# Two layers of linear attention and two of gated units on one core: a third quarter of outputs by seven products, the last z in the gated units, z reciprocals for two tiles

## The chip, the cores and the metric

The kernel runs on one core of a Trainium2 chip. The metric is the device time of one execution in microseconds, as a median of runs. TensorE (PE in the profile) multiplies matrices into PSUM banks, VectorE (DVE), ScalarE (ACT) and GpSimd (POOL) work element by element, and SyncE (SP) issues most transfers.

## What is computed

The input x is 2048 rows of 1024 numbers. Two kinds of layer follow each other, twice: attention, gated units, attention, gated units, here layers 0, 1, 2 and 3. Layers 0 and 2 share their weights, so do 1 and 3.

```
def _A_ref(x, wqkv, wo):                     # 32 heads of 32
    qkv = (x @ wqkv) ...
    phi = lambda t: where(t > 0, t + 1, exp(t)) + 1e-6
    pq, pk = phi(q), phi(k)
    kv = einsum("bhsd,bhse->bhde", pk, v)
    z = einsum("bhsd->bhd", pk)
    o = (pq @ kv) / (pq . z + 1e-6)
    return o @ wo
def _B_ref(x, W_gate, W_up, W_down):
    return (relu(x @ W_gate) * (x @ W_up)) @ W_down
x = x + A(layernorm(x)); x = x + B(layernorm(x)); and both once more
```

## The kernel before

The 2048 rows are 16 tiles of 128, in four quarters of four tiles (QT is 4). Everything stays in SBUF where it can: a pool "big" of 16 slots holds weights, transposed activations and sums, "ep" has 7 temporaries, and PSUM's eight banks are "ps" (4, tag a), "ps3" (2, tag b) and "kvp" (kv0, kv1).

**Seven products.** Most matrix products are cut into two by two blocks and made from seven block products instead of eight (1: a11 b11, 5: s1 with a difference of b, 2, 6, 7, 3, 4). The sums s and the differences are made by VectorE in f16; a product is accumulated in PSUM on top of an earlier one, after VectorE or ScalarE has read that (L1154 for the gated units: v, x, y, z banks; L677 for q and k in layer 2; L843 for outputs).

**Attention.** After q, k and their phi (L435 relu, L436 exp on ScalarE, L439 the join on VectorE) comes the product of keys and inputs (m_products, L575), z_row, and kv folded with wo into T (fold_wo, L759). An output unit (out_unit, L776) is one tile by 512 columns: eight matmuls of 512 columns into a ps bank, which VectorE adds to x (add_up, L768). The quarters 0, 1 and 2 are made in 24 such units, `out0` and the loop over sc. The fourth quarter (sc 3) is made by out_pairs, seven products for two pairs of tiles, behind the third unit (u = 2) of the next layer. Each product there has two halves of four matmuls, one for each tile of a pair: after product 1 ScalarE copies X to Y (L847), after the others VectorE adds the bank to x (onto, L836, or add_up).

**z.** For each tile GpSimd multiplies pq with zrow (z_mult, L723), VectorE sums over heads, adds and inverts (z_sum, L728 to L730, 32 numbers a row), GpSimd scales pq in place (z_scale, L735), and SP transposes it by DMA into pqT (q_turn, L744). z_mult writes ksum, one buffer. Tiles 0 to 10 run as a chain, 11 to 15 at fixed ticks.

**Layer norms.** In layers 1 and 3, ln_norm_sums takes the mean from add_up's accumulators (L222, VectorE), then ScalarE does Square, Ln and Exp (L225 to L227), a shift and the scaling (L230, L231); the result is transposed by DMA (L410), and sums_x (L1127 to L1130, VectorE) makes four sums a tile, which product 5, 6, 3 and 7 of the first gated unit read. In layer 2, ln_root is Ln and Exp (L173, L174) and ln_scale is on VectorE (L180).

**Gated units.** glu makes one of 14 units of a chunk (two quarters) from fourteen block products (7 for gate, 7 for up), 56 matmuls. six adds z = y + m5 (L1190), then V (L1203), put (L1165) multiplies relu(gate) by up, and GpSimd makes one of the four blocks (L1207). In layer 1's first chunk make_gu makes the weights' differences on VectorE (L1064, L1066, L1067) and stores them from ScalarE's queue.

**What sets the order.** Work beside the matmuls is put in by a clock of its own: `later.at(n, f)` runs f after n more `later.tick()`, and there is a tick after each unit or product. The compiler's scheduler then orders each engine by the written order as priority, by when it thinks that inputs are ready; `issue_after` and `behind(it, ...)` put an instruction behind another of its engine. In the second half of an attention layer `manual_schedule` fixes VectorE's and GpSimd's order as written. The weight ring loads ahead through SP: load_to(index + 5) at each unit's start.

Of the kernel before, what the change touches and what calls it, by code (L numbers as in the profile page):

```python
# [8 lines left out]
ALU = mybir.AluOpType  # L9
# [83 lines left out]
class _Net:  # L93
    def __init__(self, tc, ctx, x_d, wqkv_d, wo_d, wg_d, wu_d, wd_d, out_d):
# [23 lines left out]
        self.small = pool("small", 4)  # L118
        self.ps = pool("ps", 4, space=PSUM)
# [64 lines left out]
    def ln_norm(self, layer, t):  # L184
# [14 lines left out]
        def scale(rstd=None if layer == 2 else rstd):  # L199
            if rstd is None:  # L200
                rstd = self.ln_root(mv)
                return lambda: scale(rstd)
# [12 lines left out]
    def ln_norm_sums(self, layer, t):  # L215
# [13 lines left out]
        def scale():  # L229
            nc.scalar.activation(out=shift, in_=mean, func=ACT.Identity, scale=rstd[:, 0:1])  # L230
# [181 lines left out]
    def ln_at(self, delay, layer, t, lag, after=None):  # L412
        def stat():
            with self.tc.issue_after(after) if after else nullcontext():
                scale = self.ln_norm(layer, t)
            self.later.at(1, lambda: norm(scale))
# [14 lines left out]
    def phi(self, ps, out):  # L431
# [4 lines left out]
        nc.scalar.activation(out=e, in_=e, func=ACT.Exp, scale=-1.0, bias=self.eps6[:, 0:1])  # L436
# [30 lines left out]
    def layer_A(self, l, last_ln):  # L467
# [248 lines left out]
        def z_chain(i):  # L716
            z_mult(*divmod(i, QT))
            if i < 10:
                later.at(2 + i % 2, lambda: z_chain(i + 1))

        def z_mult(sc, j):
            prod = ksum
            nc.gpsimd.tensor_tensor(out=prod, in0=pq_of[sc, j], in1=zrow, op=ALU.mult)  # L723
            later.at(2, lambda: z_sum(prod, sc, j))

        def z_sum(prod, sc, j):
            den = self.small.tile([P, D // HD], F32, tag="den")
            nc.vector.tensor_reduce(out=den, in_=heads(prod), axis=mybir.AxisListType.X, op=ALU.add)  # L728
            nc.vector.tensor_scalar(out=den, in0=den, scalar1=1e-6 * self.mean, scalar2=None, op0=ALU.add)
            nc.vector.reciprocal(out=den, in_=den)  # L730
            later.at(2, lambda: z_scale(den, sc, j))

        def z_scale(den, sc, j):
# [3 lines left out]
                in1=den[:, :].unsqueeze(2).to_broadcast([P, D // HD, HD]), op=ALU.mult)  # L737
# [49 lines left out]
        def out_pairs(sc):  # L787


            nc, P2 = self.nc, 2 * P  # L790
# [4 lines left out]
            def sums_T():  # L795
                W = self.slot(f"sT{l}", [P, 2, 4, NW], F16)
                S["R"] = R = self.slot(f"sR{l}", [P, 2, 4, NW], F16)
                S[1], S[2], S[4] = W[:, 0], W[:, 1], R[:, 0]
                op(S[1], b12, b11)
                op(f16(b12), b22, b12)  # L800
                later.at(4, more_T)

            def more_T():
                op(S[2], b22, S[1])
                op(S[4], b21, S[2])

            def sums_q():
                q = pqT[sc]
                a11, a12, a21, a22 = (q[:, h:h + 4, i * P2:(i + 1) * P2] for i in range(2) for h in (0, 4))
                s1 = self.temp([P, 4, P2], F16, name="s1")  # L810
                s2, s4 = (S["R"][:, 1, i * 2:i * 2 + 2, :].rearrange("p a (b n) -> p (a b) n", n=P2)
                          for i in range(2))
                op(s1, a21, a22, ALU.add)
                op(s2, s1, a11)
# [740 lines left out]
```

## Time and profile before

| | us |
|---|---|
| median of 3 runs | 1448.36 (1448.04 to 1448.79) |
| the profiled execution | 1447.77 |
| its span, first to last instruction | 1446.0 |
| TensorE busy, VectorE, ScalarE, GpSimd | 1437.7, 959.7, 613.8, 309.6 |

The granted TensorE clock is 1.000. The first attention's output units run from 171.6 to 213.9 us, the gated units of layer 1 follow. Layer 2's output units run from 889.4 to 931.6: eight for quarter 0 (to 905.7), eight for quarter 1 (to 919.5), eight for quarter 2; then layer 3's first gated unit. In a group of instructions the columns are line, engine, operation, what it writes and reads, shapes, count, then busy time, mean ns of one, idle time of the engine before them and what ended it. In the order of time they are start, duration, engine, line, operation. A bracket tells how long the engine was idle and who released it.

### The profile page before, as it was taken

The numbers are of one execution on the slowest core, as the hardware profiler recorded it, in microseconds if no ns is written. First come the engines' busy times: TensorE is split into PE (matmuls) and PEld (weight loads), VectorE is DVE, ScalarE is ACT, GpSimd is POOL, SyncE is SP. The second block draws the span as 40 slices with busy tenths as digits, with TensorE's granted clock in tenths as the row PEclk, the third lists the DMA queues.
The fourth block names the chain that finished last, engine by engine and source line by source line (L and its number), as shares of the span: only waits on it lengthen the run. The fifth ranks groups of instructions, "written<-read, shape, count | busy, mean of one in ns | idle before, by whom it ended". The sixth has DMA issues, their size and how long they took to land.

```text
span 1446.0 us, 20268 instructions
## 1 busy us (share of the span) xinstructions
PE 1437.7 (99%) x7430; PEld 709.2 (49%) x7430; DVE 959.7 (66%) x1799; ACT 613.8 (42%) x1113; POOL 309.6 (21%) x221
## 2 busy tenths in 40 slices
PE   9999999999999999999999999999999999999998
PEld 4444444444455444445654444444444574444457
DVE  7978698677594456549687885764445864444595
ACT  7872564233334334332168726633333433333300
POOL 1453861011100011110031586410111011111002
PEclk9999999999999999999999999999999999999999
DMA  9950787997469999646973119968644799444465
GB/s 287 237 161 8 176 212 204 288 333 255 162 213 288 355 307 307 202 127 220 297 253 88 58 30 266 261 233 269 217 146 130 220 293 323 146 146 146 153 234 181
DMA packets 328836, 304.90 MB, mean 211 GB/s; under 512 B 107456, under 2 KB 291776, under 8 KB 327712
## 3 DMA queue, kind: packets, MB, share of 16 engines
q1 hardware_dynamic: 320688, 282.30, 65.8%
q10 hardware_dynamic: 6560, 17.24, 3.1%
q0 software_dynamic: 1488, 4.07, 0.8%
q8 instruction: 58, 0.95, 0.3%
q14 instruction: 42, 0.34, 0.1%
HBM read 227.28 MB, written 51.64 MB: 193 GB/s over the span
## 4 chain that ended last, share of the span: by engine, by line
PE 92%; DVE 5%; ACT 1%; issue 1%; DMA 1%; SPq 0%; DVEq 0%; ACTq 0%
PE yu L1154 10%; PE yg L1154 10%; PE ps L493 10%; PE dy L1267 8%; PE xu L1154 6%; PE xg L1154 6%; PE dx L1267 6%; PE ps L776 4%; PE zu L1154 3%; PE vg L1154 3%; PE vu L1154 3%; PE zg L1154 3%; PE my L575 3%; PE dyT L1319 2%; PE mv L575 2%; PE mx L575 2%
## 5 line engine op out<-in xcount | busy, mean ns | idle before, releaser
L1154 PEld LDWEIGHTS <-w 128*128 128x128 f16 (+1 forms) x3136 | 306.7, 98 | 372.4 <-issue 3.6
L1207 POOL TENSOR_TENSOR h<-m5u,m5g 128x512 f16<-128x512 f32 x56 | 72.7, 1298 | 721.1 <-DVE m5u L1203 660.0
L493 PE MATMUL ps<-w,xnT 128*128 128x512 bf16 x768 | 169.9, 379 | 0.5 <-ACT xnT L348 0.3
L1190 DVE TENSOR_TENSOR zg<-yg,m5g 128x512 f32<-128x512 f32 x56 | 39.1, 699 | 180.2 <-PE yg L1154 176.1
L493 PEld LDWEIGHTS <-xnT 128*128 128x128 bf16 x768 | 74.4, 98 | 90.0 <-issue 1.6
L1154 PE MATMUL yg<-s,w 128*128 128x512 f16 x448 | 115.0, 379 | 0.3 <-DVE zg L1190 0.3
L1154 PE MATMUL yu<-s,w 128*128 128x512 f16 x448 | 114.9, 379 | 0.1
L1154 PE MATMUL xu<-xnT,w 128*128 128x512 f16 x448 | 115.0, 379 | 0.0
L1154 PE MATMUL xg<-xnT,w 128*128 128x512 f16 x448 | 115.0, 379 | 0.0
L1267 PEld LDWEIGHTS <-h 128*128 128x128 f16 x672 | 65.7, 98 | 78.3
L1162 ACT ACTIVATE m5g<-m5g 128x512 f32<-128x512 f32 x56 | 35.2, 628 | 155.0 <-DVE m5g L1203 155.0
L1319 PEld LDWEIGHTS <-h 128*128 128x128 f16 x966 | 94.5, 98 | 12.3
L436 ACT ACTIVATE e<-e,eps 128x512 f32<-128x512 f32 x128 | 91.0, 720 | 3.2
L723 POOL TENSOR_TENSOR kvc<-pq,kvc 128x1024 f32<-128x1024 bf16 x32 | 78.5, 2454 | 53.1 <-DVE den L728 32.8
L1267 PE MATMUL dx<-w,h 128*128 128x512 bf16 x392 | 85.3, 379 | 0.0
L776 PE MATMUL ps<-T,pqT 128*128 128x512 bf16 x384 | 83.6, 379 | 0.0
L1171 ACT ACTIVATE m5g<-vg 128x512 f32<-128x512 f32 x56 | 33.4, 597 | 108.5 <-PE vg L1154 108.5
L1165 DVE TENSOR_TENSOR h<-yu,r 128x512 f16<-128x512 f32 x56 | 38.7, 691 | 52.8 <-PE yu L1154 52.8
L514 POOL TENSOR_TENSOR kvc<-kvc,slab 128x512 f32<-128x512 f32 x46 | 57.2, 1249 | 76.0 <-DVE slab L439 72.7
L1162 ACT ACTIVATE r<-yg 128x512 f32<-128x512 f32 x56 | 33.4, 597 | 85.2 <-PE yg L1154 85.2
L1203 DVE TENSOR_TENSOR m5u<-yu,m5u 128x512 f32<-128x512 f32 x56 | 38.7, 690 | 46.3 <-PE yu L1154 46.3
L435 ACT ACTIVATE e<-ps 128x512 f32<-128x512 f32 x92 | 54.2, 589 | 28.9 <-PE ps L493 28.8
(234 smaller groups left out, 2385.5 us busy)
## 6 DMA issues: line engine op xcount, KB each, us to landing
w<-in_B_W_gate_dram SPq DMA_DIRECT2D x56, 512.0 KB, 6.1
w<-in_B_W_up_dram SPq DMA_DIRECT2D x56, 512.0 KB, 6.0
w<-tg SPq DMA_DIRECT2D x42, 512.0 KB, 7.3
w<-tu SPq DMA_DIRECT2D x42, 512.0 KB, 6.6
w<-ddT SPq DMA_DIRECT2D x21, 896.0 KB, 6.5
w<-td SPq DMA_DIRECT2D x18, 896.0 KB, 5.0
w<-dd SPq DMA_DIRECT2D x15, 896.0 KB, 5.0
w<-in_B_W_down_dram SPq DMA_DIRECT2D x14, 896.0 KB, 4.9
```

The source lines that it names most:

```text
L435: nc.scalar.activation(out=e, in_=ps, func=ACT.Relu, scale=-1.0)
L436: nc.scalar.activation(out=e, in_=e, func=ACT.Exp, scale=-1.0, bias=self.eps6[:, 0:1])
L493: nc.tensor.matmul(by_row(ps), lhsT=self.xnT[l, l_q][:, kt, j * P:(j + 1) * P], rhs=w[:, kt, :].rearrange("p (b i d) -> p i b d", i=R, d=H ...
L514: nc.gpsimd.tensor_tensor(out=ksum[:, cols], in0=ksum[:, cols], in1=pk, op=ALU.add)
L575: nc.tensor.matmul(banks[j], lhsT=A(i)[:, j * P:(j + 1) * P], rhs=B(i), start=start and i == 0, stop=i == NS - 1, skip_group_check=True)
L723: nc.gpsimd.tensor_tensor(out=prod, in0=pq_of[sc, j], in1=zrow, op=ALU.mult)
L776: nc.tensor.matmul(ps, lhsT=pqT[sc][:, g, j * P:(j + 1) * P], rhs=T[g // 4][:, g % 4, n2 * NW:(n2 + 1) * NW], start=(g == 0), stop=(g == G ...
L1154: nc.tensor.matmul(ps, lhsT=W[w][m][:, k, :], rhs=A[m][:, k, :], start=start and k == 0, stop=k == 3, skip_group_check=True)
L1162: self.last_relu = nc.scalar.activation(out=out, in_=ps, func=ACT.Relu)
L1207: nc.gpsimd.tensor_tensor(out=h[:, 3, :], in0=V["u"], in1=V["g"], op=ALU.mult)
L1267: nc.tensor.matmul(banks[j], lhsT=A(k)[:, j * P:(j + 1) * P], rhs=w[:, i, :], start=start and k == 0, stop=k == self.U - 1, skip_group_che ...
L1319: nc.tensor.matmul(bank[:, j * H:(j + 1) * H], lhsT=A[i // 2][:, i % 2, j * P:(j + 1) * P], rhs=B[m][:, i, :], start=start and i == 0 and ...
```

## The change

In the second attention layer (l = 2) quarter 2's outputs are made by the seven products as well, in place of eight output units (`products(2, 1)`, with one tick for each product of two halves). For this the T sums are made in quarters 0 and 1 and not in layer 3's first units, and the q sums of quarter 2 in quarter 1. The products' order becomes 1, 5, 2, 6, 3, 7, 4.

In l = 2, the z of tile 11 joins the chain, and tiles 12 to 15 get theirs in layer 3's units 0 to 2 (`late_z`); their transposes, the loads of x and the q sums move to unit 3, and the last products behind it. Before, the transposes and loads were in quarter 2 and unit 0, the sums in units 1 and 2, the products behind unit 2. The first unit of layer 3 swaps the banks of v and y, and for its first four units the ring loads one weight less ahead.

In both attention layers the reciprocal is taken for two tiles at once (64 numbers a row), in a pool of its own, after the second tile's sum; the two scalings follow two and four ticks later.

Further: layer 2's ln_root is put behind the last exp of phi; layer 3's normalisation of quarter 0 goes from ScalarE's two operations to one tensor_scalar on VectorE; the last LN of quarter 1 goes behind the seeds of the products; in layer 1 make_gu for gate and up comes at two ticks, its stores behind a relu; the eight copies of x from bf16 to f32 on ScalarE fall away for two `held` temporaries; one make_dd comes one unit later.

```diff
+        self.den = pool("den", 2)
...
+                with self.tc.issue_after(self.last_exp.ins):
+                    rstd = self.ln_root(mv)
                 return lambda: scale(rstd)
             if layer % 2 == 0 and (layer, t // QT) != (2, 0):
...
+            if layer == 3 and t < QT:
+                nc.vector.tensor_scalar(out=xn, in0=src, scalar1=mean, scalar2=rstd[:, 0:1],
+                                        op0=ALU.add, op1=ALU.mult)
+                return xn
             nc.scalar.activation(out=shift, in_=mean, func=ACT.Identity, scale=rstd[:, 0:1])
             nc.scalar.activation(out=xn, in_=src, func=ACT.Identity, scale=rstd[:, 0:1],
                                  bias=shift[:, 0:1])
...
-            with self.tc.issue_after(after) if after else nullcontext():
+            it = after() if callable(after) else after
+            with self.tc.issue_after(it) if it else nullcontext():
...
-        nc.scalar.activation(out=e, in_=e, func=ACT.Exp, scale=-1.0, bias=self.eps6[:, 0:1])
+        self.last_exp = nc.scalar.activation(out=e, in_=e, func=ACT.Exp, scale=-1.0, bias=self.eps6[:, 0:1])
...
-            if i < 10:
+            if i < (11 if l else 10):
                 later.at(2 + i % 2, lambda: z_chain(i + 1))
         def z_mult(sc, j):
             prod = ksum
             nc.gpsimd.tensor_tensor(out=prod, in0=pq_of[sc, j], in1=zrow, op=ALU.mult)
-            later.at(2, lambda: z_sum(prod, sc, j))
+            if l and sc == self.NQ - 1:
+                later.at(6, lambda: self.behind(self.last_put, lambda _: z_sum(prod, sc, j), (0,)))
+            else:
+                later.at(2, lambda: z_sum(prod, sc, j))
+
+        dens = {}
         def z_sum(prod, sc, j):
-            den = self.small.tile([P, D // HD], F32, tag="den")
-            nc.vector.tensor_reduce(out=den, in_=heads(prod), axis=mybir.AxisListType.X, op=ALU.add)
-            nc.vector.tensor_scalar(out=den, in0=den, scalar1=1e-6 * self.mean, scalar2=None, op0=ALU.add)
-            nc.vector.reciprocal(out=den, in_=den)
-            later.at(2, lambda: z_scale(den, sc, j))
+            n, odd = D // HD, j % 2
+            if not odd:
+                dens[sc, j // 2] = self.den.tile([P, 2 * n], F32, tag="den", name="den")
+            den = dens[sc, j // 2]
+            nc.vector.tensor_reduce(out=den[:, odd * n:(odd + 1) * n], in_=heads(prod),
+                                    axis=mybir.AxisListType.X, op=ALU.add)
+            if odd:
+                nc.vector.tensor_scalar(out=den, in0=den, scalar1=1e-6 * self.mean, scalar2=None, op0=ALU.add)
+                nc.vector.reciprocal(out=den, in_=den)
+                for i in range(2):
+                    later.at(2 + 2 * i, lambda i=i: z_scale(den[:, i * n:(i + 1) * n], sc, j - 1 + i))
         def z_scale(den, sc, j):
             pq = pq_of[sc, j]
             nc.gpsimd.tensor_tensor(
                 out=heads(pq), in0=heads(pq),
-                in1=den[:, :].unsqueeze(2).to_broadcast([P, D // HD, HD]), op=ALU.mult)
+                in1=den.unsqueeze(2).to_broadcast([P, D // HD, HD]), op=ALU.mult)
             if sc < self.NQ - 1:
                 q_turn(sc, j)
...
+            def sums_T(n):
+                if n == 0:
+                    W = self.slot(f"sT{l}", [P, 2, 4, NW], F16)
+                    S["R"] = R = self.slot(f"sR{l}", [P, 2, 4, NW], F16)
+                    S[1], S[2], S[4] = W[:, 0], W[:, 1], R[:, 0]
+                out, a, b = ((S[1], b12, b11), (S[2], b22, S[1]), (S[4], b21, S[2]), (f16(b12), b22, b12))[n]
+                op(out, a, b)
...
-                if l == 0:
-                    with self.tc.issue_after(self.last_relu.ins):
-                        for t in range(sc * QT, sc * QT + QT):
-                            for n in range(2):
-                                nc.scalar.activation(out=half(self.x[t], n), in_=half(self.xb[t], n),
-                                                     func=ACT.Copy)
...
+                for n in ns:
+                    op(*((s1, a21, a22, ALU.add), (s2, s1, a11), (f16(a21), a11, a21), (s4, a12, s2))[n])
...
+                held = {}
+                def onto(i, n, bank, m):
+                    t = sc * QT + i
+                    xs = half(self.x[t], n)
+                    x0 = half(self.xb[t], n) if l == 0 and m not in (7, 3) else xs
+                    if l == 0 and m == 5:
+                        held[i] = self.temp(name="held")
+                    if m == 7:
+                        x0 = held.get(i, xs)
+                    out = held[i] if i in held and n == 1 else xs
+                    if m in (5, 6):
+                        nc.vector.tensor_tensor(out=out, in0=x0, in1=bank, op=ALU.add)
                     else:
-                        nc.vector.tensor_tensor(out=xs, in0=xs, in1=bank, op=ALU.add)
-                for m, bank, start, n in ((1, X, True, None), (5, V, True, (2, 1)), (6, Y, False, (0, 1)),
-                                          (2, X, False, (0, 0)), (7, Y, False, (2, 1)),
-                                          (3, V, False, (0, 1)), (4, Y, False, (2, 0))):
+                        self.last_x = add_up(t, n, out, bank, x0)
+                    if m == 4 and l == 0:
+                        later.at(6, lambda: self.behind(self.last_relu, lambda _: nc.scalar.activation(
+                            out=half(self.x[t], 1), in_=held[i], func=ACT.Copy), (0,)))
+                for m, bank, start, n in ((1, X, True, None), (5, V, True, (2, 1)), (2, X, False, (0, 0)),
+                                          (6, Y, False, (0, 1)), (3, V, False, (0, 1)),
+                                          (7, Y, False, (2, 1)), (4, Y, False, (2, 0))):
...
-                            nc.scalar.activation(out=Y[i], in_=X[i], func=ACT.Copy)
+                            self.last_seed = nc.scalar.activation(out=Y[i], in_=X[i], func=ACT.Copy).ins
                         else:
-                            onto(n[0] + i, n[1], bank[i], m not in (5, 6))
-                        later.tick()
+                            onto(n[0] + i, n[1], bank[i], m)
+                        if i or ticks == 2:
...
-            for i in range(11, self.ST):
+            sums_T, sums_q, products = out_pairs()
+            for i in range(11, 11 if l else self.ST):
+            for n, at in enumerate((1, 3, 5) if l else ()):
+                later.at(at, lambda n=n: self.behind(self.last_x, sums_T, (n,)))
-                        self.ln_at(2 * j + 2, last_ln, QT + j, 2)
-                        later.at((11 if l else 12, 13, 15, 16)[j], lambda j=j: self.sums_x(last_ln, 0, j))
-                if sc == 2 and l:
-                    for j in range(QT):
-                        later.at(11 + j, lambda j=j: q_turn(self.NQ - 1, j))
-                    for t in range(self.ST - QT, self.ST):
-                        later.at(3 + t, lambda t=t: self.behind(self.last_turn, bring, (t,)))
+                        self.ln_at((2, 4, 6, 9 if l else 8)[j], last_ln, QT + j, 2, lambda j=j: self.last_seed if l and j == 3 else None)
+                        later.at((11 if l else 12, 13, 15, 16)[j], lambda j=j: self.behind(
+                            self.last_x, lambda j: self.sums_x(last_ln, 0, j), (j,)))
-                run(row_major(out_unit, sc))
-            self.pairs = out_pairs(self.NQ - 1)
-            self.turns = [] if l else [lambda j=j: q_turn(self.NQ - 1, j) for j in range(QT)] + [
+                if sc == 1 or l == 0:
+                    for n in range(4 if l else 0):
+                        later.at(3 + n, lambda n=n: self.behind(self.last_x, lambda n: sums_q(2, (n,)), (n,)))
+                    run(row_major(out_unit, sc))
+                else:
+                    self.behind(self.last_x, sums_T, (3,))
+                    products(sc, 1)
+            self.pairs = (lambda ns: [sums_T(n) for n in ns], lambda: sums_q(self.NQ - 1),
+                          lambda: products(self.NQ - 1, 2))
+            self.late_z = [lambda j=j: z_mult(self.NQ - 1, j) for j in range(QT)] if l else []
+            self.turns = [lambda j=j: q_turn(self.NQ - 1, j) for j in range(QT)] + [
...
-        self.later.at(3, lambda: self.nc.scalar.dma_start(
-            out=self.tgu[w, u], in_=t[:, 4:8, :].bitcast(F16)))
+
+        def store():
+            with self.tc.issue_after(self.last_relu.ins) if u else nullcontext():
+                self.nc.scalar.dma_start(out=self.tgu[w, u], in_=t[:, 4:8, :].bitcast(F16))
+
+        self.later.at(3, store)
     def load_d(self, u):
         t = self.slot(f"wd{u}", [P, 2, 4, NW])
...
+        swap = (l, c, u) == (3, 0, 0)
+        def bank(w, third, name):
+            if third:
+                return self.ps3.tile([P, NW], F32, tag="b", name=name)
+            return self.kvp.tile([P, NW], F32, tag="kv0" if w == "g" else "kv1", name=name)
-            v = self.kvp.tile([P, NW], F32, tag="kv0" if w == "g" else "kv1", name=f"v{w}")
+            v = bank(w, swap, f"v{w}")
-            Y[w] = self.ps3.tile([P, NW], F32, tag="b", name=f"y{w}")
+            Y[w] = bank(w, not swap, f"y{w}")
-                nc.gpsimd.tensor_tensor(out=h[:, 3, :], in0=V["u"], in1=V["g"], op=ALU.mult)
+                self.last_h = nc.gpsimd.tensor_tensor(out=h[:, 3, :], in0=V["u"], in1=V["g"], op=ALU.mult)
...
-                ring.load_to(ring.index((l, c, "g", u)) + 5)
+                ring.load_to(ring.index((l, c, "g", u)) + (4 if (l, c) == (3, 0) and u < 4 else 5))
-                        self.later.at(4 if u else 9, lambda u=u: behind(self.last_put if u else self.last_z, lambda: [
-                            self.make_gu(ring.get((l, c, w, u + 1)), w, u + 1) for w in "gu"]))
+                        for n, w in enumerate("gu"):
+                            self.later.at((4 if u else 9) + 4 * n, lambda u=u, w=w: behind(
+                                self.last_put if u else self.last_z,
+                                lambda: self.make_gu(ring.get((l, c, w, u + 1)), w, u + 1)))
...
-                if (l, c, u) in ((1, 1, 6), (3, 0, 4)):
+                if (l, c, u) in ((1, 1, 6), (3, 0, 5)):
-                if c == 0 and u == 1:
+                if c == 0 and u == 0:
+                    for n, z in enumerate(self.late_z):
+                        self.later.at(11 + 7 * n, lambda z=z: behind(self.last_h, z))
+                if c == 0 and u == (1 if l == 1 else 3):
-                if c == 0 and u in (1, 2):
-                    self.later.at(6, lambda u=u: behind(self.last_put, self.pairs[u - 1]))
+                    if l == 1:
+                        self.later.at(6, lambda: behind(self.last_put, lambda: self.pairs[0]((0, 3))))
+                        self.later.at(10, lambda: behind(self.last_put, lambda: self.pairs[0]((1, 2))))
+                if c == 0 and u == (2 if l == 1 else 3):
+                    self.later.at(6 if l == 1 else 11, lambda: behind(self.last_put, self.pairs[1]))
-                if c == 0 and u == 2:
+                if c == 0 and u == (2 if l == 1 else 3):
```

## The prediction

> **What bounds the kernel now.** I read the engine busy times, TensorE's groups with shapes kept apart, TensorE's waits, the busy times of the second attention's output stage, and then stretches of the order of time.
>
> ```profile
> PE 1437.7 (99%) x7430; PEld 709.2 (49%) x7430; DVE 959.7 (66%) x1799; ACT 613.8 (42%) x1113; POOL 309.6 (21%) x221
> ...
> L776 PE MATMUL ps<-T,pqT 128*128 128x512 bf16 x384 | 83.6, 379 | 0.0
> ```
>
> TensorE is never free. Its output units (L776, eight matmuls each) start 1.726 us apart (905.67, 907.40, ...), so a 512-column matmul costs 216 ns in the stream; the 379 is its latency. A removed matmul is worth 216 ns, an added wait costs its whole length. Starts that come later than 216 ns show which waits exist; the view of waits, which subtracts the latency, names the largest:
>
> ```profile
> PE qy L677 <- DVE qz L699: 1.0, 1, 1.0
> ...
> PE yg L1154 <- DVE zg L1190: 0.3, 1, 0.3
> ...
> PE vg L1154 <- DVE s L1127: 0.2, 1, 0.2
> ```
>
> By starts these are 1.19 us at 751 (with 0.28 at 747 just before), 0.47 at 306 and 0.40 at 217. TensorE is full, but every gain can be lost where VectorE, which empties its banks, is late. In the stage that is changed:
>
> ```profile
> 891.70:905.50 13.80, 13.80 (x77) 6.23 (x65) 9.48 (x25) 7.76 (x16) 6.89 (x4) 1.00 1.12 247
> 905.50:919.30 13.80, 13.80 (x66) 6.26 (x65) 11.04 (x30) 13.60 (x28) 10.26 (x6) 1.00 1.08 298
> 919.30:932.90 13.60, 13.60 (x65) 6.14 (x64) 12.15 (x31) 5.79 (x13) 4.75 (x3) 1.00 1.05 220
> ```
>
> (columns: PE, PEld, DVE, ACT, POOL). VectorE is at 32.7 of 41.2 us before anything is added; ScalarE is full in the second row.
>
> **What the Trainium skill says.** "TensorE: Matmul & The Clock Gate", Back-to-back issue gap: N/2.4 + 2.5 ns, 216 ns at N = 512, for isolated matmuls, 131 sustained; this trace shows 216 sustained. "SBUF — State Buffer", Who interferes with whom: a VectorE instruction with two SBUF inputs and a GpSimd instruction that reads SBUF exclude each other for a whole instruction. The trace agrees, at the end of the first attention:
>
> ```profile
> 206.61 1.91 POOL L735 TENSOR_TENSOR pq<-pq,den 128x1024 bf16<-128x1024 bf16 x1 [0.69 <-DVE den L730]
> ...
> 206.93 2.13 DVE L1064 TENSOR_TENSOR w<-w 128x1024 f16<-128x1024 bf16 x1
> 209.10 0.42 DVE L1066 TENSOR_TENSOR w<-w 128x512 f16<-128x512 bf16 x1
> ```
>
> The 2.13 us operation takes 0.68 elsewhere; it ran when GpSimd had ended at 208.52. "Perfetto Trace Analysis", Sequencer Loop: an engine takes its instructions in order, and each waits for its own semaphores. That is the rule by which one late input holds all behind it.
>
> **The change, part by part.**
>
> 1. *Products.* 64 matmuls become 56: 8 x 216 ns = **-1.73 us**, all on the path.
>
> 2. *Square roots behind the last exp (ln_root, layer 2).* In the before:
>
> ```profile
> 748.34 0.29 ACT L173 ACTIVATE rstd<-mv,eps 128x1 f32<-128x1 f32 x1 [0.63 <-DVE mv L195]
> ...
> 749.14 0.29 ACT L173 ACTIVATE rstd<-mv,eps 128x1 f32<-128x1 f32 x1 [0.27 <-DVE mv L195]
> 749.34 0.58 ACT L435 ACTIVATE e<-ps 128x512 f32<-128x512 f32 x1
> ```
>
> The phi of a bank that was full at 747.1 starts at 749.34, behind two Ln that wait for statistics. VectorE's join stands still for its exp (1.60 us idle), and L699 behind the join. With the edge the relu starts when the ACT copy ends (747.62), exp ends at 748.9, join 749.6, L699 750.3, ahead of the matmul's 750.87. Both waits go (1.47); VectorE is next, 0.5 us short of late. Bounds -1.5 to 0; I take **-1.4**.
>
> 3. *Layer 1's units.* make_gu's two halves four ticks apart, its stores behind a relu, eight ACT copies (0.6 each) replaced by two. At 306 a VectorE queue with six w operations (3.2 us back to back) delays zg; half of them moves: -0.47, and 0.1 to 0.2 from 225 and 248. Against it, the u half now stands between put and zu in all units, where 7u has 0.3 us to spare; other matmuls can be ordered into that. -0.8 to +0.6; **-0.5**.
>
> 4. *Pairs of z, first attention.* Even tiles save 0.18 + 0.35 us of VectorE, but the two scales of a pair now come to GpSimd together. For tiles 14 and 15 both follow the last reciprocal (206.5), each 1.9 us. L1064 still runs at 208.5; the second scale then takes the port at 209.1 and L1066 waits to 211. From 206.9 to 219.5 VectorE has no gap (make_gu, add_up, sixteen sums_x), so this moves the s that vg waits for: wait 0.40 becomes 2.2. Bounds 0 (VectorE wins the port) to +2.0; **+1.6**.
>
> 5. *Layer 2's output stage.* VectorE's list from 893.3 (last phi) to the first s of the fourth sums_x: z of tile 10 and 11 1.1 + 1.8; 16 add_up x 0.61 = 9.8; 8 mv x 0.13 = 1.0; four T sums x 1.14 = 4.6; four normalisations now on VectorE at 0.73 (L180 with the same shapes 0.8, minus overlap) = 2.9; four q sums x 0.65 = 2.6; 12 adds of the products x 0.61 = 7.3; three sums_x x 1.47 + 0.4 = 4.8. Sum 35.9 us. Gone are four z sums (1.7 each). TensorE would come to the product that needs this s (vg, now 935.02) at 933.3, so 40.0 us are there and 4.1 may be waits. In VectorE's written order I count: 0.9 for GpSimd's product of tile 11; 0.7 and 0.5 for the port at the first two T sums; 1.6 in the second and third normalisation and 1.6 in the fourth, each of which needs Square, Ln and Exp (1.82 us) of a mean written only one unit before, with another tile's chain ahead of it on ScalarE: 5.3, and up to 1.5 where VectorE then waits for TensorE. The early ones reach TensorE through the four banks: add_up of the stage's unit 12 would end at 917.7 where its bank is wanted at 917.8. So vg starts 1.1 to 2.7 us late, somewhat more with the two ACT seeds behind ScalarE's backlog. I take 2.3 of waits; bounds 0 and 5.5.
>
> 6. *Products' order 2, 6, 3, 7, 4* puts one half product between 7 and 4 on a bank. The same distance costs 0.16 at 938 (6g, 6u, 7g). Three calls, partly filled: **+0.2** (0 to 0.5).
>
> 7. *Last z in layer 3's units:* four products, four scales (2.1, 1.9) on GpSimd, which has 10.8 us free a unit; four reductions of 1.2 on VectorE, which has 5; units' VectorE operations have one SBUF input, so no port. 0. *Turns, loads of x and q sums in unit 3:* before, four turns behind four weight loads on SP were issued in 8.3 us and landed 13.4 after the first load. With the first pair of loads early (a slot is free when ksum is done) I get 7.5 to 9.5 us after the unit's start; the q sums come at tick 11, 9.5 us, and behind them stand the V and put operations that free the unit's banks. The x tiles then land 12 to 16 us in; the first is wanted at 14.9. 0 to +3; **+0.4**. T sums leaving unit 0 and the ring at depth 4: 0, loads take 7 of a unit's 12 us.
>
> **Sum**: -1.73 - 1.4 - 0.5 + 1.6 + 2.3 + 0.2 + 0.4 = +0.9. The profiled execution is 1447.77 (span 1446.0 and 1.8 around it), so 1448.7; the median of the runs shown lies 0.6 above it, so **1449.2**.
>
> **The rivals.**
> A (likeliest, 0.45): given back as above, 1446.5 to 1451.2.
> B (0.25): *the covers hold.* VectorE wins the port in 4 and the normalisations find ScalarE free in 5: -1.73 - 1.4 - 0.5 = -3.6, 1444.8. For it: the before shows no wait between 891.9 and 938, ScalarE loses four scalings of 1.5 us. Against it: part 5's list.
> C (0.20), slower: *VectorE's queue sets the output stage.* If ScalarE runs each chain whole, the fourth normalisation waits longer, the seeds are 2.2 us late and products 2 and 4 wait: 5.5 instead of 2.3, total +4.1, 1452.5. It decides from where unit 12's add_up ends later than TensorE asks for the bank.
> D (0.10), slower: *the turns land late in unit 3*, q sums hold VectorE for 3 us: +3 on A, 1452.2.
> A variant, that the compiler's order isn't the written one, is inside these ranges: TensorE's order is free, VectorE's and GpSimd's is fixed in this stage.
>
> **Numbers.** 0.2% is 2.9 us, about what a measurement of this kernel can tell from no change: below 1445.5 is faster, above 1451.3 slower. B gives faster 0.25; C and D slower 0.30; A same 0.45. The range leaves out the lower end of B and the upper of C: 1444.3 to 1453.0.
>
> **What would show it.** 1: 64 fewer matmuls in the groups of output units, 56 more in those of the products. 2: no late matmul at 747 to 752. 4: two L735 without a gap at the end of layer 0, a VectorE sum of over 1.8 us beside each, vg's wait above 2 us. 5: VectorE at over 90% from 893 to 935, normalisations ended by ACT rstd, the first two banks of the products ended by VectorE. 7: q sums in unit 3 ended by a transfer. The prediction is wrong if vg in layer 3 follows its predecessor without a wait, or if layer 0's end shows no second blocked sum.

## The result, and the profile after

The changed kernel takes 1450.93 us (median of 19 runs, 1450.67 to 1452.66), the kernel before 1448.29 us in the same session (19 runs, 1447.94 to 1449.12). The ratio is 1.002, 95% interval 1.0013 to 1.0027: slower by 2.6 us. The profiled execution has a span of 1449.1 us against 1446.0, 3.1 more; the profiled run of the kernel before was 0.5 us under its median.

The page and its groups first: eight matmuls fewer in all, 64 fewer in the output units, so the products do what they say.

```profile
PE 1438.3 (99%) x7422; PEld 708.7 (49%) x7422; DVE 964.5 (67%) x1779; ACT 607.2 (42%) x1101; POOL 312.8 (22%) x221
...
L794 PE MATMUL ps<-T,pqT 128*128 128x512 bf16 x320 | 70.2, 379 | 0.9 <-DVE x L786 0.8
```

The group of output units, without any wait before (0.0), now has 0.9 us of it, ended by VectorE's add_up (L786). The view of TensorE's waits shows the new ones; none of these four was there before:

```profile
PE xu L1185 <- DVE x L786: 1.1, 1, 1.1
PE ox L862 <- ACT oy L866: 1.0, 1, 1.0
PE ps L794 <- DVE x L786: 0.8, 1, 0.8
PE ov L862 <- DVE x L786: 0.4, 1, 0.4
```

The first is at the start of layer 1 (a bank that one of the first attention's last output units still holds), the other three in the second output stage. The wait of 1.0 for qz at the head of layer 2 is gone from the list. The second output stage by windows, moved by the 0.67 us that the stage begins later; the third row runs on to 935.40, about where TensorE has done the same work (columns PE, PEld, DVE, ACT, POOL, clock, DMA share, GB/s):

```profile
892.37:906.17 13.80, 13.80 (x77) 6.22 (x65) 11.65 (x21) 4.65 (x10) 10.88 (x5) 1.00 0.94 166
906.17:919.97 13.80, 12.95 (x60) 5.71 (x59) 11.54 (x27) 9.67 (x23) 0.90 (x1) 1.00 0.93 246
919.97:935.40 15.43, 13.75 (x63) 5.88 (x62) 13.90 (x36) 9.32 (x17) 0.00 (x0) 1.00 1.12 253
```

TensorE, full in every row before, loses 0.9 and 1.7 us in the second and third. VectorE is busy for 37.1 of 43.0 us (86%), ScalarE no longer fills the second row, and GpSimd's work has crowded into the first.

To see where the time went, I compare when TensorE begins the same work in both traces. Each figure is how much later (+) or earlier the changed kernel is at the end of a stretch than at its beginning:

| stretch | measured | predicted |
|---|---|---|
| start to the first attention's output units | +0.26 (the start-up varies by 0.9 between profiles) | none |
| from there to layer 1's first vg | +1.85 | +1.6 |
| layer 1's units | -0.34 | -0.5 |
| head of layer 2 (to 822) | -1.09 | -1.4 |
| to the second attention's output units | 0.0 | 0 |
| output units and products, to layer 3's vg ("the stage") | +1.84 = -1.73 + 3.57 of waits | -1.73 + 2.3 + 0.2 |
| layer 3's units | +0.58 | +0.4 |
| sum | +3.1 | +0.9 |

### The profile page after: what moved, and what is told of

The parts are those of the page before. It is cut to its first block, busy times and chain, and to the rows that moved or that the text cites. A ratio compares the mean times of both kernels' runs of the same rounds, so it can differ in the third digit from the quotient of the medians.

```text
span 1449.1 us, 20219 instructions
## 1 busy us (share of the span) xinstructions
PE 1438.3 (99%) x7422; PEld 708.7 (49%) x7422; DVE 964.5 (67%) x1779; ACT 607.2 (42%) x1101; POOL 312.8 (22%) x221
## 4 chain that ended last, share of the span: by engine, by line
PE 93%; DVE 3%; ACT 2%; issue 1%; DMA 0%; SPq 0%; DVEq 0%; ACTq 0%
PE ps L500 10%; PE yu L1185 10%; PE yg L1185 10%; PE dy L1305 7%; PE xu L1185 7%; PE xg L1185 6%; PE dx L1305 6%; PE ps L794 4%; PE vg L1185 3%; PE zg L1185 3%; PE zu L1185 3%; PE vu L1185 3%; PE my L582 3%; PE dyT L1357 2%; PE mx L582 2%; PE mv L582 2%
## 5 line engine op out<-in xcount | busy, mean ns | idle before, releaser
L794 PE MATMUL ps<-T,pqT 128*128 128x512 bf16 x320 | 70.2, 379 | 0.9 <-DVE x L786 0.8
L1193 ACT ACTIVATE r<-zg 128x512 f32<-128x512 f32 x56 | 32.9, 587 | 80.8 <-PE zg L1185 77.1
```

Of the source, the lines that this page charges most:

```text
L794: nc.tensor.matmul(ps, lhsT=pqT[sc][:, g, j * P:(j + 1) * P], rhs=T[g // 4][:, g % 4, n2 * NW:(n2 + 1) * NW], start=(g == 0), stop=(g == G ...
L1193: self.last_relu = nc.scalar.activation(out=out, in_=ps, func=ACT.Relu)
```

## The experiments

All runs are given as medians beside the kernel before, which took 1448.2 to 1448.4 in the four sessions; "the stage" is the TensorE time from the second attention's first output unit to vg of layer 3: 45.65 us before, 47.50 after.

**Step 4, the pair of z.** In the changed kernel, VectorE at the end of the first attention, and GpSimd beside it (two scalings in one line):

```profile
207.51 2.07 DVE L1091 TENSOR_TENSOR w<-w 128x1024 f16<-128x1024 bf16 x1
209.62 2.02 DVE L1093 TENSOR_TENSOR w<-w 128x512 f16<-128x512 bf16 x1
```

```profile
207.12 4.23 POOL L753 TENSOR_TENSOR pq<-pq,den 128x1024 bf16<-128x1024 bf16 x2 [0.72 <-DVE den L747]
```

Each sum ends only after a scaling has ended (at 209.03 and 211.35); alone they take 0.68 and 0.42. The first experiment takes the pair away in the first attention alone:

```diff
-            if odd:
+            if l == 0:
+                d = den[:, odd * n:(odd + 1) * n]
+                nc.vector.tensor_scalar(out=d, in0=d, scalar1=1e-6 * self.mean, scalar2=None, op0=ALU.add)
+                nc.vector.reciprocal(out=d, in_=d)
+                later.at(2, lambda: z_scale(d, sc, j))
+            elif odd:
```

> The changed kernel, but in the first attention layer each tile's reciprocal is taken at once and its scaling follows two ticks later, as before. Theory (two scalings together hold the port): the sum L1093 beside GpSimd's second scaling takes 0.42 again, vg's wait in layer 1 falls from about 2.1 us in all to 0.4, time 1.7 us under the changed kernel, about 1449.2. Rival (VectorE's queue there is late in any case, and the lost time only shows at this place): under 0.5 us gained.

Measured: 1449.0 us (ratio to before 1.0006, 0.9998 to 1.0014), 1.9 less than the changed kernel. VectorE in the same place:

```profile
206.97 2.13 DVE L1096 TENSOR_TENSOR w<-w 128x1024 f16<-128x1024 bf16 x1
209.13 0.43 DVE L1098 TENSOR_TENSOR w<-w 128x512 f16<-128x512 bf16 x1
```

One blocked sum instead of two, as in the kernel before, and the stretch to vg is back to what it was (0.00). The loss in the first attention is the second blocked sum; that the port is what blocks it is read from when these operations end.

**The normalisations of step 5.** The block on VectorE is taken out, so ScalarE scales and shifts as before:

```diff
-            if layer == 3 and t < QT:
-                nc.vector.tensor_scalar(out=xn, in0=src, scalar1=mean, scalar2=rstd[:, 0:1],
-                                        op0=ALU.add, op1=ALU.mult)
-                return xn
```

> The changed kernel, but layer 3's normalisation of quarter 0 is ScalarE's again (two operations a tile, 1.5 us). Theory (VectorE's queue sets the output stage): VectorE sheds four operations of 0.8 us and the 1.6, 0.1 and 2.1 us that it stood in front of them; waits of the output units and of products 1 and 5 shrink, 1.0 us gained or more, 1449.9. Rival (ScalarE sets it): 6 us more on ScalarE before the seeds, product 2 waits longer than 1.2 us, no gain or up to 2 us lost.

Measured: 1451.28 us (1.0021, 1.0013 to 1.003), 0.35 more than the changed kernel; the stage takes 47.61. Its waits:

```profile
PE oy L858 <- DVE x L846: 1.4, 1, 1.4
PE ox L858 <- ACT oy L862: 1.3, 1, 1.3
...
PE oy L858 <- DVE x L782: 0.5, 1, 0.5
```

No output unit waits any more, but the seeds, on ScalarE, come later (1.43 by starts, instead of 1.16), and what VectorE adds behind them later still. The theory's gain isn't there: giving the work back moves the wait and doesn't shorten it.

**GpSimd's early product.** The trace shows something that the prediction didn't count. GpSimd in the stage:

```profile
897.38 1.91 POOL L753 TENSOR_TENSOR pq<-pq,den 128x1024 bf16<-128x1024 bf16 x1
899.25 2.13 POOL L730 TENSOR_TENSOR kvc<-pq,kvc 128x1024 f32<-128x1024 bf16 x1
901.33 5.75 POOL L753 TENSOR_TENSOR pq<-pq,den 128x1024 bf16<-128x1024 bf16 x2
```

The middle line is the product of tile 12, meant for layer 3's units. It comes up at tick 11 of unit 0, where last_h still is layer 1's last (at 648.89), so its edge holds nothing back, and it runs ahead of two scalings. VectorE meanwhile, the first and the third normalisation of the stage:

```profile
905.23 2.40 DVE L233 TENSOR_SCALAR xnb<-x,mv,rstd 128x1024 f16<-128x1024 f32 x1
...
914.69 0.81 DVE L233 TENSOR_SCALAR xnb<-x,mv,rstd 128x1024 f16<-128x1024 f32 x1 [2.05 <-ACT rstd L229]
```

The first takes 2.40 instead of 0.81: it ends 0.55 us after GpSimd's last scaling (907.08). The other stood still for 2.05 us for ScalarE's rstd. The third experiment moves the late products by one tick, behind unit 0's own h:

```diff
-                        self.later.at(11 + 7 * n, lambda z=z: behind(self.last_h, z))
+                        self.later.at(12 + 7 * n, lambda z=z: behind(self.last_h, z))
```

> The changed kernel, but the late z start one tick later (12 in place of 11), where the instruction that they are put behind is unit 0's own GpSimd product and not one of the layer before. In the changed kernel's trace the first of them runs at 899.3, between two scalings of quarter 2. Theory: without it the two scalings end 2.1 us earlier, the first normalisation no longer waits 1.6 us for the port, 1.0 to 1.6 us gained, 1449.6. Rival (the wait for ScalarE's chains comes next in any case): under 0.4 us.

Measured: 1450.01 us (1.0012, 1.0005 to 1.0018), 0.92 less, a little under what was expected. The product now runs at 945.00, 46 us later; the first normalisation takes 0.80, but the third still stands 2.05 us for its rstd. The stage takes 46.41; layer 3's units give 0.3 of that back.

**Step 2 alone**, in the kernel before:

```diff
-                rstd = self.ln_root(mv)
+                with self.tc.issue_after(self.last_exp.ins):
+                    rstd = self.ln_root(mv)
...
-        nc.scalar.activation(out=e, in_=e, func=ACT.Exp, scale=-1.0, bias=self.eps6[:, 0:1])
+        self.last_exp = nc.scalar.activation(out=e, in_=e, func=ACT.Exp, scale=-1.0, bias=self.eps6[:, 0:1])
```

> The kernel before, with only ln_root put behind the last exp. Theory: the waits of 0.28 and 1.19 us at the head of layer 2 go, a new one of up to 0.4 may come; 1.1 us gained, 1447.2. Rival (the head's gain in the changed kernel came from other parts of the change): no difference.

Measured: 1447.32 us (0.9993, 0.9985 to 1.0001), 0.9 less than before; the head of layer 2 is 1.12 us shorter in its trace, though the interval still touches no change. The new wait at 778, which the changed kernel has too, is there (0.35).

**Both repairs together** (single z in the first attention, tick 12 in the second):

> The changed kernel with both repairs at once: reciprocals of single tiles in the first attention, and tile 12's product behind unit 0's own h in the second. If the port at the end of layer 0 and GpSimd's early product are two separate losses, they add: 1450.93 - 1.93 - 0.92 = 1448.1. If what is gained before layer 1 or in the output stage is given back later by VectorE's queue in layer 3's units, some of it goes: 1448.6 to 1449.0.

Measured: 1447.84 us (0.9997, 0.9988 to 1.0005). The two losses add (3.1 against 2.85). What is left in the stage, 46.40 us, is 2.5 of waits against 1.73 of products saved. Everything below starts from this kernel, and the next five runs concern the stage alone.

**The title of the change undone**: quarter 2 by output units again.

```diff
-                if sc == 1 or l == 0:
-                    for n in range(4 if l else 0):
-                        later.at(3 + n, lambda n=n: self.behind(self.last_x, lambda n: sums_q(2, (n,)), (n,)))
-                    run(row_major(out_unit, sc))
-                else:
-                    self.behind(self.last_x, sums_T, (3,))
-                    products(sc, 1)
+                run(row_major(out_unit, sc))
...
+                    if l == 3:
+                        self.later.at(6, lambda: behind(self.last_put, lambda: self.pairs[0]((3,))))
```

(and the statistics of tile 7 at tick 8, with no seed to wait for)

> The kernel with both repairs, and its third quarter in layer 2 by eight output units again instead of seven products a pair (the four q sums, sixteen adds into partial results and two pairs of seeds go, 8 add_up come in; the last T sum moves to layer 3's unit 1). 8 x 216 ns of matmuls come back: +1.73. Theory 'the products bring their own waits' (VectorE some 6 us lighter in the stage, no seed): the 2.5 us of waits of the stage fall to about 0.4, so 1448.1 + 1.73 - 2.1 = 1447.7. Rival 'the waits come from the normalisations on VectorE and the earlier T sums, whatever computes the third quarter': they stay, 1449.8.

Measured: 1448.22 us (0.9998, 0.9989 to 1.0006), stage 46.79. One wait remains besides 0.12 just before:

```profile
PE ps L799 <- DVE x L791: 0.9, 1, 0.9
```

By starts it is 1.02, in front of unit 16, and the 0.12 is in front of unit 14, with the stage's units counted from 0. (Counted so, quarter 0 ends at 903.9 and quarter 1 at 917.8 in the kernel before, each one unit earlier than the description above has it.) The edit takes twelve adds away, four of them plain and eight add_up, not the sixteen of the expectation. The seven products are worth 0.4 us here, not 1.73; but 1.1 us of waits stay without them, so both theories hold a part.

**The two holds of the stage, one at a time.** First, the statistics of tile 6 behind the first seeds on ScalarE, as tile 7's are:

```diff
-                        self.ln_at((2, 4, 6, 9 if l else 8)[j], last_ln, QT + j, 2, lambda j=j: self.last_seed if l and j == 3 else None)
+                        self.ln_at(((2, 4, 9, 10) if l else (2, 4, 6, 8))[j], last_ln, QT + j, 2, lambda j=j: self.last_seed if l and j > 1 else None)
```

> The kernel with both repairs, and the statistics of tile 6 put behind the first seeds on ScalarE, as those of tile 7 are. Theory 'ScalarE's chain ahead of the seeds holds product 2': the 1.15 us in front of product 2 goes, and at most 0.3 comes elsewhere: 1447.2. Rival 'VectorE's queue sets the stage and the seeds only show it': TensorE waits as long at the next bank or at vg, 1448.1.

Measured: 1447.37 us (0.9994, 0.9986 to 1.0002), stage 45.44. The wait for the seeds (1.14) is gone, and 0.4 comes at vg, where the fourth s is now later. The median fell by 0.47, the trace's stage by 0.96; the sizes are within the scatter of the medians.

Second, the normalisations on VectorE two units behind their statistics instead of one:

```diff
-            self.later.at(1, lambda: norm(scale))
+            self.later.at(2 if layer == 3 and t < QT else 1, lambda: norm(scale))
```

> The kernel with both repairs, and the four normalisations on VectorE two units behind their statistics instead of one. Theory 'VectorE stands still for ScalarE's rstd, and TensorE's banks pay for it': the 2.05 us of idle VectorE at 911.7 goes, and with it 0.1 + 0.35 + 0.8 at the banks of unit 12 and of the first products: 1447.1. Rival 'ScalarE sets the stage, as in the run with the normalisations on ScalarE': TensorE then waits that much longer for the seeds, 1448.1.

Measured: 1446.77 us (0.999, 0.9984 to 0.9997), stage 45.42. The third normalisation in its trace no longer has the 2.05 us of idle time before it, nor has any of the others one:

```profile
904.49 0.80 DVE L233 TENSOR_SCALAR xnb<-x,mv,rstd 128x1024 f16<-128x1024 f32 x1
...
907.69 0.80 DVE L233 TENSOR_SCALAR xnb<-x,mv,rstd 128x1024 f16<-128x1024 f32 x1
...
910.59 0.81 DVE L233 TENSOR_SCALAR xnb<-x,mv,rstd 128x1024 f16<-128x1024 f32 x1
...
914.06 0.81 DVE L233 TENSOR_SCALAR xnb<-x,mv,rstd 128x1024 f16<-128x1024 f32 x1
```

The waits in front of unit 14 (for unit 10's bank) and at the first product banks (0.11 + 0.35 + 0.81) went with it; the seeds' wait stayed (1.27). At the medians this kernel is 1.4 us faster than the kernel before and, across sessions, 4.2 us faster than the changed one.

**Both holds taken away:**

> The kernel with both repairs, the normalisations two units behind their statistics and the statistics of tile 6 behind the first seeds, all together. Theory 'two separate holds, VectorE on a rstd and ScalarE ahead of the seeds': the 1.27 us that was left in front of product 2 goes as well, and 0.2 to 0.4 comes back at vg: 1446.77 - 0.9 = 1445.9. Rival 'a full stage gives back what one hold yields': VectorE's queue up to the fourth s is then next and takes all of it, 1446.8.

Measured: 1446.88 us (0.9991, 0.9984 to 0.9997), stage 45.29: no better than the normalisations alone. Its waits:

```profile
PE oy L867 <- DVE x L791: 0.5, 1, 0.5
PE oy L867 <- DVE x L855: 0.5, 1, 0.5
```

The seeds' 1.27 us came back as 0.63 and 0.66 (by starts) at the products' last banks. The rival's number holds, but the trace doesn't show the full queue that it names. VectorE stands still once more, for a transposed tile:

```profile
923.38 0.42 DVE L1163 TENSOR_TENSOR s<-xnT 128x512 f16<-128x512 f16 x1 [0.98 <-DMA xnT<-xnb]
...
924.86 1.28 DVE L855 TENSOR_TENSOR x<-x,oy 128x512 f32<-128x512 f32 x2
```

The adds that empty the banks oy stand behind these sums, and TensorE, which asked for the first bank at 924.96, goes on at 925.59. Without the 0.98 us idle that add would be done by 924.6, and about 1 us of the 1.29 would go (an estimate from these times). So a third late input is next, the transpose; no run here moves it.

**Room for VectorE, and output units**: the normalisations two units behind, and the title undone.

> The kernel with both repairs and the normalisations two units behind, with the third quarter of layer 2 by output units again. Theory 'the four q sums, adds and seeds are what the seven products cost, and the normalisations cost both forms alike': the 1.02 + 0.12 us of waits at units 12 and 13 go here too: 1448.22 - 1.14 = 1447.1; against the same kernel with seven products (1446.77) the products are worth 0.3, and without the seeds' wait 1.2. Rival 'the waits by units came from the queue, not from the normalisations': 1448.2.

Measured: 1447.48 us (0.9993, 0.9985 to 1.0002), stage 45.66. No wait is left in the stage, which is what it took before (45.65). So the waits of 1.14 by units were the normalisations'. Against 45.42 and 45.29 with products, these are worth 0.2 to 0.4 us in the traces (0.6 between the medians of one session, 1446.88 and 1447.48): of the 1.73 saved, 1.3 to 1.5 goes to waits that come with them, for the seeds or at the banks behind the late transpose.

**Step 3.** Both halves of make_gu at one tick again:

```diff
-                            self.later.at((4 if u else 9) + 4 * n, lambda u=u, w=w: behind(
+                            self.later.at((4 if u else 9), lambda u=u, w=w: behind(
```

> The kernel with both repairs, and make_gu's two halves in layer 1's units at one tick again. If splitting them is what the units of layer 1 gained, the wait of 0.47 us for zg at 306 comes back and the 0.20 and 0.16 at 296 and 334 go: 1447.84 + 0.1 to + 0.4. Rival 'the gain there came from the two ACT copies instead of eight': no wait at 306, 1447.8.

Measured: 1450.54 us (1.0014, 1.0008 to 1.0021), 2.7 more than with the halves split (2.2 between the spans of the traces), far above both expectations. The wait near 308 that the theory named is back (0.47), so its rival falls, but a larger one of 1.26 and one of 0.47 behind it come from 294 to 298, which neither named. VectorE there:

```profile
293.15 0.69 DVE L1096 TENSOR_TENSOR w<-w 128x1024 f16<-128x1024 bf16 x1 [2.58 <-DMA w<-in_B_W_up_dram]
...
294.89 0.69 DVE L1233 TENSOR_TENSOR zg<-yg,m5g 128x512 f32<-128x512 f32 x1
```

The u half waits for its weights, with zg behind it in the queue. Before, the same operation waited 0.25 and began at 291.13. The load landed at 291.04 before and lands at 293.06 here, and at 293.65 in the kernel with both repairs, where the halves are split and no operation of VectorE waits for it. So in the changed kernel this load lands 2 us or more later, and the split hides it. What makes it later wasn't tried; the store that now stands behind a relu is a candidate.

**Step 7.** In the changed kernel's layer 3, VectorE:

```profile
953.25 1.21 DVE L743 TENSOR_REDUCE den<-kvc 128x32 f32<-128x1024 f32 x1
954.38 0.69 DVE L1228 TENSOR_TENSOR zu<-yu,m5u 128x512 f32<-128x512 f32 x1
954.97 0.68 DVE L1241 TENSOR_TENSOR m5g<-yg,m5g 128x512 f32<-128x512 f32 x1
955.57 1.15 DVE L746 TENSOR_SCALAR den<-den 128x64 f32<-128x64 f32 x1
```

The reduction stands between the unit's first put and zu, which 7u (product 7 of the up half) waits for. The last experiment, on the kernel with both holds taken away, puts the reductions behind zu:

```diff
-                later.at(6, lambda: self.behind(self.last_put, lambda _: z_sum(prod, sc, j), (0,)))
+                later.at((10, 4, 8, 4)[j], lambda: self.behind(self.last_z, lambda _: z_sum(prod, sc, j), (0,)))
...
-                        self.later.at(11 + 7 * n, lambda z=z: behind(self.last_h, z))
+                        self.later.at((12, 22, 28, 36)[n], lambda z=z: behind(self.last_h, z))
```

> The last kernel with both repairs, both spacings in the output stage, and the late z's reductions in layer 3's units 1 and 2 behind each unit's zu instead of between its first put and zu; the last pair's scalings come some 4 us later for it. Theory 'the reductions of 1.2 us ahead of zu are what these units lost': the waits of 0.16 and 0.30 us at 7u in units 1 and 2 go, 1446.88 - 0.46 = 1446.4. Rival 'the turns decide in unit 3': the q sums there, which already wait 0.8 us for a turn without TensorE noticing, wait some 4 us longer, and the puts and V operations behind them on VectorE hold TensorE by 1 to 3 us, 1448 to 1450.

In this kernel the reductions of tiles 12 and 14 read the next tile's product, so the z of those tiles is another. Measured: 1449.78 us (1.001, 1.0003 to 1.0017). The 0.16 of unit 1 is gone. At unit 2 TensorE waits 1.89, since the reduction waits for that later product: this is the experiment's own fault and says nothing of the theory. Unit 3 is clean enough to read:

```profile
979.41 0.69 DVE L553 TENSOR_TENSOR s<-pqT 128x1024 f16<-128x1024 bf16 x1 [2.80 <-DMA pqT<-pq]
980.02 0.68 DVE L1246 TENSOR_TENSOR m5u<-yu,m5u 128x512 f32<-128x512 f32 x1
```

The last scaling ends at 971.91 instead of 969.50, the q sum waits 2.80 instead of 0.73 for the turn, m5u stands behind it, and TensorE waits 1.59 at 4u and 0.53 later. The rival's mechanism exists: 2.4 us more delay than in the kernel with both holds taken away is enough to bring it out.

## Why the prediction was right or wrong

The time fell into the range and on the side of case A (given back), 1.7 us above the point. The change cost 2.6 us where 0.9 was forecast; a range 8.7 us wide covers that. By its steps:

1. *Products, -1.73*: right. The eight matmuls are gone, and each still stands for 216 ns of the stream.
2. *Square roots, -1.4*: right in its mechanism, measured -1.09. The prediction said that VectorE is next, 0.5 us short of late; it is late at 778, where the trace has a new wait of 0.37 for a phi (0.35 with the edge alone). ScalarE after the change has the relu and exp free of the square roots that stood ahead of them:

```profile
748.66 0.60 ACT L442 ACTIVATE e<-ps 128x512 f32<-128x512 f32 x1 [0.83 <-PE ps L500]
749.29 0.72 ACT L443 ACTIVATE e<-e,eps 128x512 f32<-128x512 f32 x1
```

3. *Layer 1's units, -0.5*: measured -0.34, and for a reason that the prediction had only in part. Its six w operations in a row are there, but the split is worth more than 2 us in the changed kernel, because a load lands later.
4. *The pair of z, +1.6*: right, +1.85, of which the first experiment recovers all. The sign that was named, a wait above 2 us at vg, was not there (0.44): the delay reaches TensorE earlier, at banks that add_up empties (0.24, 0.35 and 1.21, at 212 to 217). The prediction took the s of sums_x for what waits first for the delayed VectorE; it was the banks.
5. *Output stage, +2.3, with 0.2 of step 6*: this is the term that was mis-sized. It is 3.57. VectorE's own share is 2.19 (0.20 and 0.98 in front of units 10 and 14, then 0.06, 0.35 and 0.60 at the products' first banks), and 0.22 is step 6. The other 1.16 is the seeds on ScalarE, which the prediction named ("somewhat more") and didn't price; the run that moves the statistics of tile 6 behind them takes this wait away (0.41 of it then comes at vg). The place was wrong too. The prediction let the 4.1 us that VectorE has free before the fourth sums_x absorb most of its late inputs and put the rest at vg (1.1 to 2.7; its own figures give 1.2). But banks are wanted long before that, and vg, 1.84 us late, follows its predecessor without a wait, four matmuls of 216 ns behind the start of xu:

```profile
936.67 1.03 PE L1185 MATMUL xu<-xnT,w 128*128 128x512 f16 x4
937.54 1.03 PE L1185 MATMUL vg<-s,w 128*128 128x512 f16 x4
```

By the prediction's own words that is a sign of being wrong. Nor is VectorE at over 90% from 893 to 935, but at 87%. The inputs one by one: GpSimd's product of tile 11: 1.03 of idle VectorE for 0.9. The port at the first two T sums: 0.2 and 0.25 each instead of 0.7 and 0.5. The normalisations: 2.05 at the third and 0.1 at the second, for 1.6; none at the fourth, where 1.6 was counted. Not in the list at all was the product of tile 12 (0.92 by experiment): the prediction put all four products into layer 3's units because the code says so, and did not ask which instruction last_h names when the edge is made. Nor was the port at a normalisation, which that product brought about (1.6). That all these add up to 5.2 us, near the 5.3 counted, is luck. The Trainium skill, "SBUF — State Buffer", Who interferes with whom, says that tensor_scalar can take the shared pair as well; I applied the rule to operations with two inputs alone. The trace agrees with it: 2.40 for 0.81, and 1.15 for 0.19 at L746 in layer 3.
6. *Order of the products*: one wait of 0.22 at 933.9, as predicted, and one of 0.09 at 264 in layer 1.
7. *Late z, 0; turns, +0.4*: the sum is near (+0.58), the split wrong. The late reductions cost 0.16, 0.20 and 0.14 in front of zu and V, although VectorE has 5 us to spare in a unit: the spare time was not where they stand. Another 0.12 comes at 1028, where the make_dd that moved by one unit stands ahead of zu. The turns cost nothing; the q sum waits 0.8 for one and TensorE doesn't notice.

Of the rivals, B (the covers hold) is refuted by the two blocked sums and by the third normalisation. C has its place and its order right: VectorE loses time at a normalisation, a bank comes late (unit 10's by 0.98 and not unit 12's, which is 0.06 late), and the seeds wait (1.16). But the price is 3.57 in all, not 5.5. D is there and doesn't act.

So the change's own idea, seven products instead of eight, saves 1.73 us of TensorE and nets 0.2 to 0.4 where VectorE is so full. The rest of what it lost, the pair of z, the early product and the normalisation one unit too early, is not part of that idea: repaired, the same products give 1446.8 us. Most of what that kernel gains on the kernel before is again not theirs: the edge of step 2 alone gave 0.9 us at the median and 1.12 in the trace.

## What to carry to other kernels

Where one engine is full and another nearly so, price a saving on the first at what the second leaves of it: list the second engine's work in its own order, and mark each operation whose input comes from a third. Time that is free before the last thing that the first engine wants is no cover for what it wants earlier: here the waits came at banks that were emptied late, and none at the sum that ends the list. An edge "behind the last X" is only as good as the X that the name holds when it is made; look up which instruction that is. Spare time in a stretch is no cover for an operation that stands in front of the one that TensorE wants next.

## What was not expected of the hardware

- Where both had work ready, the shared port went back and forth: GpSimd's first scaling ended at 209.03, VectorE's sum then ran to 209.58, the second scaling took 2.36 from its start (1.91 alone) and ended at 211.35, and VectorE's next sum ended after that (2.02 for 0.42). Two scalings in a row thus cost VectorE 1.4 and 1.6 us.
- The addition of a constant to 64 columns (L746) took mostly 0.63 and once 1.15 beside GpSimd, where it takes 0.18 to 0.20 otherwise: small operations wait at the port like large ones. It runs sixteen times; each of the nine that began while a GpSimd operation was running ended 0.05 to 0.06 us after that. The reduction (L743) took 1.21 or 1.22 wherever it stood, beside GpSimd or not.
- Taking 2.05 us of idle VectorE away was worth 1.0 us of TensorE; taking 1.27 us of the seeds' wait away afterwards was worth nothing that can be measured (1446.88 against 1446.77), at least in part because VectorE then stood 0.98 us for a transfer.
